# Loading batch 3's x earlier, and a new order around batch 2's scores and normalisation

## The chip, the core and the metric

The kernel runs on one core of a Trainium2 chip. The core has four engines that compute: TensorE (PE in the profile; PEld is its weight load), VectorE (DVE), ScalarE (ACT) and GpSimd (POOL). SyncE (SP) computes nothing here; it issues DMAs, as GpSimd and ScalarE also do. Each engine takes its own instructions strictly in order, and waits for the others by semaphores. TensorE writes its results to PSUM, of which the kernel uses two pools of four banks; VectorE and ScalarE carry them on to SBUF.

The metric is the device time of one execution in microseconds. The kernel before takes 205.47 us, the median of six runs (205.08 to 206.97).

## What is computed

Two blocks follow each other: a cross attention between a sequence and a small state, and a feed-forward layer with the exact GELU. Cut to what matters:

```python
B, H, S, Ns, D = 8, 8, 512, 32, 64
# x [B,H,S,D], state [B,H,Ns,D], w_in [512,2048], w_out [2048,512], all float32
a     = softmax(x @ state.T / sqrt(D))       # over the 32 states
xread = a @ state
a2    = softmax(state @ x.T / sqrt(D))       # over the 512 positions
sread = a2 @ x
X     = concat([xread, sread], axis=2)       # [B, H, S+Ns, D] -> [B*(S+Ns), H*D]
out   = gelu(X @ w_in) @ w_out               # [4352, 512]
```

## The kernel before

**What is tiled how.** Everything stays in bfloat16 between the steps. The work goes by batch, 0 to 7, 512 positions each. For a batch the kernel forms the transposed x (`xT`), multiplies it with the states (`scores`: 16 small matmuls in two halves, each followed by one exp on ScalarE), normalises on VectorE (`norm`: a sum, a reciprocal and a product for each half) and transposes the result (`AT`). It never forms xread: `p_mm` multiplies the states with w_in into `P` (by `f`, blocks of 512 columns), and the first layer is AT times P. `M(k)` (`mm1`) is one of its 128-column chunks of a batch: two matmuls into a PSUM tile `hp`, then one GELU on ScalarE into `g`. There are 16 chunks for a batch, so M(16) to M(31) belong to batch 1 and M(32) begins batch 2.

The second layer is `U` (`mm2`) for batch 0: output rows j, evacuated by VectorE into `osb` and written by SyncE. From batch 1 on it is `X`, a scheme with seven products over halves (named "1" to "7"), whose operands are sums of g (`g_sum`) or of w_out (`w_sums`), formed on VectorE.

**What sets the order.** The program is written out by hand. Each engine executes its instructions in the order in which they stand in the program, and waits are derived from the tiles. So a line's place decides what it stands behind on its engine, and the pools decide what it can wait for:

- `xin` has two buffers of `xb`, the loaded x: batch 3's x uses the buffer of batch 1, whose last readers are `xtr(1)` on TensorE and `rearr_ones(1)` on VectorE.
- `ps_f` is a ring of four PSUM banks (`ftile`): hp, the scores' `pt`, most P tiles and the transposed states pass through it in turn.
- `ps_o` has four banks named o0 to o3 (`otile`): the output rows of U and the products of X. X "3" and "5" share bank 0, "4" and "2" bank 1, "1" and "7" bank 2, and "6" has bank 3.

**The stage around the change** lies between the end of batch 0's second layer and the regular loop over batches 2 to 7 (L1112). There GpSimd's queue is: `load_rest` (the rest of the weights, the states of batch 2, the x of batch 2, and as the last piece w_out's chunks 12 to 15), then `rearr(2)` (two copies that arrange x into `x4`, the form that can be transposed by DMA), a small copy `hold_for(0, 15)` that makes the queue wait for a GELU of batch 0, `load_x(3)`, `load_st(3, B)` (the states of batches 3 to 7), `rearr(3, (0,))`, a copy that waits for batch 2's normalised scores, `rearr(3, (1,))`, another hold and `rearr_ones(2)`.

SyncE's queue is: `xtr_dma(2)` (the DMA that transposes x4 into xT), the writes of U(12) to U(15), `atr_dma(2)` (the transpose of batch 2's normalised scores `a` into AT), `xtr_dma(3)`.

TensorE's order is: M(18, 19), U(12), P for batch 1, U(13), states of batch 2, M(20, 21), U(14), M(22, 23), U(15), scores of batch 2, X(1, "3"), M(24) to M(27), X(1, "6"), P for batch 2 (`p0`, `p1`), M(28) to M(31), the transposed states of batches 3 to 7 (`state_prep(3, B)`, which needs `load_st(3, B)`), and then M(32).

On ScalarE two table loads stand around the exps of each batch: one from GELU to exp, one back.

Of the kernel before, what the change touches and what calls it, by code (L numbers as in the profile page):

```python
# [9 lines left out]
FP32 = mybir.dt.float32  # L10
BF16 = mybir.dt.bfloat16
AF = mybir.ActivationFunctionType
# [5 lines left out]
def kernel(  # L18
# [8 lines left out]
    nc = tc.nc  # L27
# [11 lines left out]
    persist = ctx.enter_context(tc.tile_pool(name="persist", bufs=1))  # L39
# [36 lines left out]
    xT0 = persist.tile([128, 4, SJ, 128], BF16, name="xT0", tag="mix2")  # L76
    sb0 = persist.tile([128, 2, 2, 2, NS], BF16, name="sb0")
    hold = persist.tile([128, 1], BF16, name="hold")
    warm = persist.tile([128, 512], BF16, name="warm")
    xos = [persist.tile([128, SJ, HC, 132], BF16, name=f"xo_{i}") for i in range(2)]  # L80
    x4s = [persist.tile([128, SJ, HC, 128], BF16, name=f"x4_{i}") for i in range(2)]
# [15 lines left out]
    for i in range(2):  # L97
        nc.vector.memset(xos[i][:, :, :, 1:2], 1.0)
        nc.vector.memset(xos[i][:, :, :, 130:131], 1.0)

    def load_w_in(f0, f1):
        for t in range(2):
            nc.gpsimd.dma_start(
                out=w_in_bf[64 * t:64 * t + 64, :, f0:f1],
                in_=moe_w_in[256 * t:256 * t + 256, f0:f1].rearrange("(c d) f -> d c f", c=HC),
            )
# [3 lines left out]
    def load_w_out(m0, m1):  # L110
        nc.gpsimd.dma_start(out=w_out_bf[:, m0:m1, :], in_=w_out_r[:, m0:m1, :])

    def load_x(b):
        xb = xin.tile([128, H, SJ * D], BF16, name="xb", tag="xb")
        nc.gpsimd.dma_start(out=xb, in_=xr[b])
        xbs[b] = xb

    def load_st(b0, b1):
        nc.gpsimd.dma_start(
            out=st_bf[:, b0:b1, :, :].rearrange("q b t d -> q (b t) d"),  # L120
            in_=st_rows[:, b0:b1, :, :].rearrange("q b t d -> q (b t) d"),
        )
# [9 lines left out]
    def load_rest():  # L132
        load_w_out(4, 6)
        load_w_out(6, 8)
        load_w_in(1024, 1536)
        load_w_out(8, 12)
        load_w_in(1536, 2048)
        load_st(2, 3)
        load_x(2)
        load_w_out(12, 16)  # L140


    def keep_warm(n):
# [57 lines left out]
    atts = {}  # L201

    def begin(b):
        A = Att()
        atts[b] = A
        A.x4 = x4s[b % 2]
        A.xo = xos[b % 2]
        if b > 0:
            A.xT = att.tile([128, SJ, HC, 128], BF16, name="xT", tag="xT")
# [8 lines left out]
    def rearr(b, ts=(0, 1)):  # L218
        A = atts[b]
        src = xbs[b].rearrange("p (t c) (j d) -> p t c j d", t=2, d=D)  # L220
        for t in ts:
            nc.gpsimd.tensor_copy(  # L222
                out=A.x4[:, :, :, 64 * t:64 * t + 64].rearrange("p j c d -> p c j d"),
                in_=src[:, t],
            )
# [47 lines left out]
    def xtr_dma(b):  # L273
        A = atts[b]
        nc.sync.dma_start_transpose(
            out=A.xT.rearrange("p j c n -> p (j c) n"),
            in_=A.x4.rearrange("p j c n -> p (j c n)"),
        )
# [29 lines left out]
    def norm0(t):  # L308
        A = atts[0]
        ics = att.tile([128, SJ, HC], FP32, name="ics", tag="ics")  # L310
        nc.vector.reciprocal(out=ics, in_=A.sums)
        nc.vector.tensor_tensor(
            out=A.a.rearrange("p (j t) (c n) -> p j t c n", t=2, n=NS)[:, :, t, :, :],
            in0=A.e.rearrange("p (j t) (c n) -> p j t c n", t=2, n=NS)[:, :, t, :, :],
            in1=ics[:, :, :].to_broadcast((128, SJ, HC, NS)),
            op=ALU.mult,
        )

    def scores(b, half):
        A = atts[b]  # L320
        if half == 0:
            begin_e(b)
        pt = ps_f.tile([128, SJ, 2, 2, NS], FP32, name="pt", tag="f")
        for ci in range(2):
            c = 2 * half + ci
            for j in range(SJ):
                nc.tensor.matmul(  # L327
                    pt[:, j, :, ci, :],
                    lhsT=A.xT[:, j, c, :],
                    rhs=sbd[:, b, c, :],  # L330
                    start=True,
                    stop=True,
                )
        nc.scalar.activation(  # L334
            out=A.e[:, :, 64 * half:64 * half + 64],
            in_=pt.rearrange("p j t c n -> p (j t) (c n)"),
            func=AF.Exp,
            scale=scale,
        )
# [75 lines left out]
    Ps = {}  # L415
# [128 lines left out]
    def w_add(name, x, y, op):  # L544
        if name == "3":
            pair = persist.tile([128, 2, MH, NH], BF16, name="ws_34", tag="mix0")
            w_sum["3"], w_sum["4"] = pair[:, 0], pair[:, 1]
        elif name != "4":
            tag = {"6": "mix1", "1": "mix2", "7": "mix3"}[name]
            w_sum[name] = persist.tile([128, MH, NH], BF16, name=f"ws_{name}", tag=tag)  # L550
        nc.vector.tensor_tensor(out=w_sum[name], in0=x, in1=y, op=op)

    def w_sums(i):
        (b11, b12), (b21, b22) = w_q
        w_add(*(
            ("3", b12, b22, ALU.subtract),
            ("4", b21, b11, ALU.subtract),
            ("6", b11, b12, ALU.add),
            ("1", b11, b22, ALU.add),
            ("7", b21, b22, ALU.add),  # L560
        )[i])
# [14 lines left out]
    def g_sum(b, name):  # L576
        (h0, k0), (h1, k1), op = G_SUMS[name]
        t = apool.tile([128, MH, 256], BF16, name="gsum", tag="gsum")
        nc.vector.tensor_tensor(out=t, in0=g_q(b, h0, k0), in1=g_q(b, h1, k1), op=op)  # L579
        xs[b, "g" + name] = t  # L580
# [34 lines left out]
    def X(b, name):  # L615
        bank = {"3": 0, "4": 1, "5": 0, "2": 1, "1": 2, "6": 3, "7": 2}[name]
        first = name in "3416"
        if first:
            xs[b, bank] = otile([128, 2, NH], "xp", bank)
        ps = xs[b, bank]  # L620
        lhs = {"3": (0, 0), "4": (1, 1)}.get(name)
        lhs = xs[b, "g" + name] if lhs is None else g_q(b, *lhs)
        rhs = {"5": w_q[1][1], "2": w_q[0][0]}.get(name)
        rhs = w_sum[name] if rhs is None else rhs
        x_mm(ps, lhs, rhs, first)
        if name == "3":
            xs[b, "s3"] = c_tile("s3")
            if b > 1:
                nc.scalar.copy(out=xs[b, "s3"], in_=ps)
            for h in range(2):  # L630
                xs[b, "o", h] = hpool.tile([128, 2, d_model], FP32, name="oh", tag=f"oh{h}")
        elif name == "4":
            xs[b, "s34"] = c_tile("s34")
            nc.vector.tensor_tensor(out=xs[b, "s34"], in0=ps, in1=xs[b, "s3"], op=ALU.add)
        elif name == "5":
            o = xs[b, "o", 0][:, :, NH:]
            nc.scalar.copy(out=o, in_=ps)  # L637
            xs[b, "u"] = c_tile("u")
            x_out(b, 0, right)
            nc.gpsimd.tensor_tensor(out=xs[b, "u"], in0=xs[b, "s34"], in1=o, op=ALU.subtract)  # L640
        elif name == "2":
            nc.scalar.copy(out=xs[b, "o", 1][:, :, :NH], in_=ps)  # L642
            c22(b)
        elif name == "1":
            xs[b, "q"] = c_tile("q")
            nc.vector.tensor_tensor(out=xs[b, "q"], in0=ps, in1=xs[b, "s34"], op=ALU.add)
        elif name == "7":
            nc.vector.tensor_tensor(
                out=xs[b, "o", 0][:, :, :NH], in0=ps, in1=xs[b, "u"], op=ALU.add
            )  # L650
            x_out(b, 0, left)
# [253 lines left out]
    def hold_for(b, m):  # L905
        nc.gpsimd.tensor_copy(out=hold, in_=gs[b][:, m, 0:1])


    def M(*ms):
        for m in ms:  # L910
            mm1(m // MC, m % MC)

    def U(*us):
        for u in us:
            mm2(u // 16, u % 16 // 4, u % 4)
# [146 lines left out]
    begin(2)  # L1062
    rearr(2)
    xtr_dma(2)
    hold_for(0, 15)
    load_x(3)
    load_st(3, B)
    M(18, 19)
    U(12)
# [1 line left out]
    U(13)  # L1071
    state_prep(2, 3, ps_o, "o3")
    w_sums(1)
    begin(3)
    rearr(3, (0,))
    M(20, 21)
    U(14)
    M(22, 23)
    g_sum(1, "6")
    U(15)  # L1080
    scores(2, 0)
    scores(2, 1)
# [1 line left out]
    norm(2, 0)  # L1084
    norm(2, 1)
    atr_dma(2)
    nc.gpsimd.tensor_copy(out=hold, in_=atts[2].a[:, 0, 64:65])
    rearr(3, (1,))
    xtr_dma(3)
    M(24, 25)  # L1090
    M(26, 27)
    X(1, "6")
    homes = iter((1, 2, None, None))

    def home(shape, name):
        at = next(homes)
# [1 line left out]

    p0 = p_mm(2, 0, home)
    p1 = p_mm(2, 1, home)  # L1100
    for f, t, ps in ((1, 0, p1), (1, 1, p1), (0, 1, p0)):
        nc.vector.tensor_copy(out=Ps[2][:, t, f * 512:(f + 1) * 512], in_=ps[t])
    M(28, 29)
    nc.scalar.copy(out=Ps[2][:, 0, 0:512], in_=p0[0])
    hold_for(1, 12)
    rearr_ones(2)
    M(30, 31)
    state_prep(3, B)
    nc.scalar.copy(out=xs[1, "s3"], in_=xs[1, 0])
    w_sums(3)  # L1110

    for b in range(2, B):  # L1112
# [122 lines left out]
```

The softmax here doesn't subtract the row's maximum and nothing guards it: scores larger than these inputs give would overflow.

## Time and profile before

| | |
|---|---|
| median of six runs | 205.47 us |
| the profiled execution | 205.34 us |
| its span in the profile | 203.6 us |
| granted TensorE clock | 1.00 throughout |
| DMA queue of GpSimd's loads (casting float32 to bfloat16) | 13984 packets, 8.10 MB |
| DMA queue of SyncE's writes and transposes | 25872 packets, 14.36 MB |
| HBM read, written | 17.30 MB, 8.91 MB |
| GELU on ScalarE, 128x512 | 124 of them, 602 ns each |
| table load on ScalarE | 1283 ns each |
| sum of two g blocks on VectorE, 128x2048 | 35 of them, 1326 ns each |
| rearranging copy on GpSimd, 128x1024 | 12 of them, 1081 ns each |
| x of one batch, from issue to landing | median 6.0 us |
| DMA transpose of x, of a, to landing | median 4.4 us, 3.7 us |

In the profile a line of a timeline gives the start, the length, the engine with the source line, the operation with its tiles (output <- input), and in brackets the idle time before it with what ended it. Starts are more exact than ends on TensorE, since matmuls are pipelined and their ends are modelled. A chain of waits is followed back from the last instruction to what released each step; its lines give start, length and what it was. The span is the time in which the engines run; the rest of the 205.34 us lies around it.

### The profile page before, as it was taken

The page shows a single profiled execution, that of the slowest core. Times are in us where ns is not written, and L with a number is a line of the kernel's source. Part 1 is how long each engine was busy: PE and PEld are TensorE (multiplying, and loading weights), DVE is VectorE, ACT ScalarE, POOL GpSimd, SP SyncE. Part 2 cuts the span into 40 slices and gives each one's busy share as a digit, 9 for nine tenths or more (in the row PEclk, how much of TensorE's full clock was granted, in tenths as well). Part 3 has the DMA queues.
Part 4 walks back from the last instruction along what each step waited for, and adds up shares of the span by engine and source line. Part 5 has one row for each costly group of instructions (what it writes and reads, how often), then busy time and mean ns, then how long its engine had stood idle before and what let it go on. Part 6 is the DMA issues. An engine that isn't in the chain of part 4 may idle for free.

```text
span 203.6 us, 4900 instructions
## 1 busy us (share of the span) xinstructions
PE 196.6 (97%) x2035; PEld 132.6 (65%) x2035; DVE 157.2 (77%) x254; ACT 135.4 (67%) x239; POOL 68.0 (33%) x76
## 2 busy tenths in 40 slices
PE   7699999999899999999999999999999999999994
PEld 2333544465577567766776677667776787878893
DVE  2773777688998988977897787768778988895882
ACT  3685677678986679565967697587847576864120
POOL 8972303323529546370626602330220002200000
PEclk9999999999999999999999999999999999999999
DMA  6999996994785798745583405750107001040135
GB/s 195 189 191 191 197 199 108 148 223 125 120 143 106 190 122 104 158 156 53 70 170 127 104 0 117 105 148 0 52 3 206 3 0 55 0 155 3 52 101 162
DMA packets 40566, 23.16 MB, mean 114 GB/s; under 512 B 21856, under 2 KB 39136, under 8 KB 40544
## 3 DMA queue, kind: packets, MB, share of 16 engines
q0 software_dynamic: 13984, 8.10, 29.7%
q1 hardware_dynamic: 25872, 14.36, 28.5%
q10 hardware_dynamic: 688, 0.39, 0.6%
q8 instruction: 16, 0.26, 0.5%
q14 instruction: 6, 0.05, 0.1%
HBM read 17.30 MB, written 8.91 MB: 129 GB/s over the span
## 4 chain that ended last, share of the span: by engine, by line
PE 89%; DMA 5%; ACT 3%; DVE 1%; issue 1%; SPq 0%
PE xp L585 39%; PE hp L488 25%; PE op L530 5%; PE p_ps L423 4%; PE sp L792 3%; PE rp L858 3%; DMA x0f<-in_x_dram 3%; PE xp L697 2%; PE op L514 2%; DMA AT<-a 2%; PE pt L327 1%; PE sr L386 1%; ACT g L495 1%; PE hp L1003 1%; ACT L495 1%; ACT L334 1%
## 5 line engine op out<-in xcount | busy, mean ns | idle before, releaser
L495 ACT ACTIVATE g<-hp 128x512 bf16<-128x512 f32 x124 | 67.3, 602 | 27.4 <-PE hp L488 20.8
L488 PE MATMUL hp<-AT,P 128*128 128x512 bf16 x248 | 63.0, 379 | 0.7 <-DMA AT<-a 0.7
L585 PEld LDWEIGHTS <-gsum 128*128 128x128 bf16 x528 | 51.0, 98 | 12.4 <-issue 1.9
L579 DVE TENSOR_TENSOR gsum<-g 128x2048 bf16<-128x2048 bf16 x35 | 45.9, 1326 | 0.1
L488 PEld LDWEIGHTS <-P 128*128 128x128 bf16 x248 | 22.8, 98 | 21.4 <-issue 3.2
L585 PE MATMUL xp<-ws,gsum 128*128 128x256 bf16 x304 | 36.3, 273 | 0.0
L585 PE MATMUL xp<-ws,g 128*128 128x256 bf16 x224 | 26.8, 273 | 0.0
L585 PE MATMUL xp<-w_out_bf,gsum 128*128 128x256 bf16 x224 | 26.6, 273 | 0.0
L585 PEld LDWEIGHTS <-g 128*128 128x128 bf16 x224 | 21.7, 98 | 4.6 <-issue 0.2
L640 POOL TENSOR_TENSOR u<-s,oh 128x512 f32<-128x512 f32 x6 | 8.9, 1490 | 40.7 <-ACT oh L637 40.7
L435 DVE CAST P<-p_ps 128x512 bf16<-128x512 f32 x29 | 18.8, 684 | 3.0 <-PE p_ps L423 2.9
L222 POOL COPY x<-xb 128x1024 bf16<-128x1024 bf16 x12 | 12.7, 1081 | 20.7 <-DMA xb<-in_x_dram 20.7
L434 ACT CAST P<-p_ps 128x512 bf16<-128x512 f32 x29 | 15.8, 598 | 5.4 <-PE p_ps L423 5.1
L232 POOL COPY xo<-xb 128x1024 bf16<-128x1024 bf16 x12 | 14.6, 1246 | 4.5 <-PE sr L386 4.5
L604 POOL TENSOR_TENSOR v<-q,oh 128x512 f32<-128x512 f32 x6 | 8.7, 1456 | 20.5 <-ACT oh L642 20.3
L530 PE MATMUL op<-w_out_bf,g 128*128 128x512 bf16 x48 | 11.8, 380 | 0.0
L350 DVE TENSOR_TENSOR a<-e,ics 128x512 bf16<-128x512 bf16 x14 | 10.4, 739 | 0.5
L347 DVE TENSOR_REDUCE cs<-e 128x16 f32<-128x512 bf16 x14 | 9.5, 677 | 1.1 <-ACT e L334 1.1
L423 PE MATMUL p_ps<-w_in_bf,sbd 64*32 64x512 bf16 x248 | 10.3, 382 | 0.0
L413 DVE COPY XSR<-srT 128x128 bf16<-128x128 bf16 x8 | 5.7, 757 | 5.3 <-PE srT L410 5.3
L334 ACT ACT_TABLE_LOAD x7 | 9.0, 1283 | 0.6 <-issue 0.5
L495 ACT ACT_TABLE_LOAD x7 | 9.0, 1283 | 0.1
(129 smaller groups left out, 225.0 us busy)
## 6 DMA issues: line engine op xcount, KB each, us to landing
out_dram<-oh SPq DMA_DIRECT2D x15, 256.0 KB, 2.8
xb<-in_x_dram POOLq DMA_DIRECT2D x7, 512.0 KB, 6.0
out_dram<-oh SPq DMA_DIRECT2D x6, 512.0 KB, 3.1
w_in_bf<-in_moe_w_in_dram POOLq DMA_DIRECT2D x6, 256.0 KB, 11.6
out_dram<-osb SPq DMA_DIRECT2D x5, 256.0 KB, 4.5
w_out_bf<-in_moe_w_out_dram POOLq DMA_DIRECT2D x4, 256.0 KB, 8.3
w_out_bf<-in_moe_w_out_dram POOLq DMA_DIRECT2D x2, 512.0 KB, 13.2
x0f<-in_x_dram SPq DMA_DIRECT2D x3, 256.0 KB, 3.9
```

What stands on the lines that cost most here:

```text
L222: nc.gpsimd.tensor_copy(out=A.x4[:, :, :, 64 * t:64 * t + 64].rearrange("p j c d -> p c j d"), in_=src[:, t],)
L232: eng.tensor_copy(out=A.xo[:, :, :, 2 + 64 * t:66 + 64 * t].rearrange("p j c d -> p c j d"), in_=src[:, t],)
L334: nc.scalar.activation(out=A.e[:, :, 64 * half:64 * half + 64], in_=pt.rearrange("p j t c n -> p (j t) (c n)"), func=AF.Exp, scale=scale,)
L350: nc.vector.tensor_tensor(out=A.a[:, :, hs].rearrange("p g (c n) -> p g c n", n=NS), in0=e4, in1=ics[:, :, :].to_broadcast((128, G, 2, NS) ...
L423: nc.tensor.matmul(ps[t][32 * c:32 * c + 32, :], lhsT=sbd[64 * t:64 * t + 64, b, c, 32 * t:32 * t + 32], rhs=w_in_bf[64 * t:64 * t + 64, c ...
L434: nc.scalar.copy(out=dst[:, 0, :], in_=ps[0])
L435: nc.vector.tensor_copy(out=dst[:, 1, :], in_=ps[1])
L488: nc.tensor.matmul(hp, lhsT=Ps[b][:, t, m * 128:(m + 1) * 128], rhs=atts[b].AT[:, :, t, :], start=(t == 0), stop=(t == 1),)
L495: nc.scalar.activation(out=gs[b][:, m, :], in_=hp, func=AF.Gelu)
L530: nc.tensor.matmul(ops[b, j], lhsT=gs[b][:, m, j * 128:(j + 1) * 128], rhs=w_out_bf[:, m, :], start=(m == 0), stop=(m == MC - 1),)
L579: nc.vector.tensor_tensor(out=t, in0=g_q(b, h0, k0), in1=g_q(b, h1, k1), op=op)
L585: nc.tensor.matmul(ps[:, j - js[0], :], lhsT=lhs[:, m, 128 * j:128 * j + 128], rhs=rhs[:, m, :], start=(first and j == js[0] and m == 0), ...
```

## The change

There are five parts. The load of batch 3's x moves from behind the hold to the end of `load_rest`, so that it is the next thing in GpSimd's queue after the last w_out piece; all of `rearr(3)` follows `rearr(2)` at once, and the states of batches 3 to 7 now stand behind a one-element copy that reads batch 2's xT. The transpose of batch 3's x is issued by SyncE between the writes of U(14) and U(15), no longer behind `atr_dma(2)`. M(22, 23) come ahead of U(14), and behind their GELUs stands a new exp of one element per partition (`exp_table` on `spare`). `g_sum(1, "6")` moves behind batch 2's normalisation on VectorE, and `X(1, "6")` behind the transposed states on TensorE. The four P tiles of batch 2 get other banks (three of ps_o and one of the ring), and ScalarE casts the last of them and VectorE the other three.

```diff
+    spare = persist.tile([128, 1], FP32, name="spare")
...
+    nc.vector.memset(spare, 0.0)
...
         load_st(2, 3)
         load_x(2)
         load_w_out(12, 16)
+        load_x(3)
...
+    def exp_table():
+        nc.scalar.activation(out=spare, in_=spare, func=AF.Exp)
...
     begin(2)
     rearr(2)
     xtr_dma(2)
-    hold_for(0, 15)
-    load_x(3)
+    begin(3)
+    rearr(3)
+    nc.gpsimd.tensor_copy(out=hold, in_=atts[2].xT[:, 0, 0, 0:1])
     load_st(3, B)
     M(18, 19)
     U(12)
...
     U(13)
     state_prep(2, 3, ps_o, "o3")
     w_sums(1)
-    begin(3)
-    rearr(3, (0,))
     M(20, 21)
+    M(22, 23)
+    exp_table()
     U(14)
-    M(22, 23)
-    g_sum(1, "6")
+    xtr_dma(3)
     U(15)
     scores(2, 0)
     scores(2, 1)
...
     norm(2, 0)
     norm(2, 1)
     atr_dma(2)
-    nc.gpsimd.tensor_copy(out=hold, in_=atts[2].a[:, 0, 64:65])
-    rearr(3, (1,))
-    xtr_dma(3)
+    g_sum(1, "6")
     M(24, 25)
     M(26, 27)
-    X(1, "6")
-    homes = iter((1, 2, None, None))
+    homes = iter((1, 3, 2, None))
...
     p0 = p_mm(2, 0, home)
     p1 = p_mm(2, 1, home)
-    for f, t, ps in ((1, 0, p1), (1, 1, p1), (0, 1, p0)):
+    nc.scalar.copy(out=Ps[2][:, 1, 512:1024], in_=p1[1])
+    for f, t, ps in ((0, 1, p0), (0, 0, p0), (1, 0, p1)):
         nc.vector.tensor_copy(out=Ps[2][:, t, f * 512:(f + 1) * 512], in_=ps[t])
     M(28, 29)
-    nc.scalar.copy(out=Ps[2][:, 0, 0:512], in_=p0[0])
     hold_for(1, 12)
     rearr_ones(2)
     M(30, 31)
     state_prep(3, B)
     nc.scalar.copy(out=xs[1, "s3"], in_=xs[1, 0])
+    X(1, "6")
     w_sums(3)
```

## The prediction

> **What bounds the kernel now.** I read the page's busy shares first, then who waited for whom on the PE, then the chain of work in order of time around the changed stage. From the page:
>
> ```profile
> PE 196.6 (97%) x2035; PEld 132.6 (65%) x2035; DVE 157.2 (77%) x254; ACT 135.4 (67%) x239; POOL 68.0 (33%) x76
> ```
>
> The PE (TensorE) is the bound, nearly without a gap. The list of PE waits has four lines; all but one lie in the first 15 us. The one in the steady part:
>
> ```profile
> PE hp L488 <- DMA AT<-a: 0.7, 1, 0.7
> ```
>
> The chain from 38 to 58 us shows where it sits (start, length, what):
>
> ```profile
> 42.60 0.47 issue
> 43.07 1.28 ACT L334
> 44.35 0.01 issue
> 44.37 1.08 ACT e L334 x2
> 45.45 0.02 issue
> 45.47 1.28 ACT L495
> 46.75 0.01 issue
> 46.76 1.70 ACT g L495 x4
> 48.47 3.35 DMA AT<-a
> 51.82 0.04 issue
> 51.86 1.02 PE hp L488 x4
> ```
>
> For 9 us the chain leaves the PE: batch 2's scores end, ACT waits, loads the exp table (1.28), runs two exps, AT is transposed by DMA, and only then can M(32) start. From 45.47 to 48.47 it names ACT's GELUs, which run beside it; the transpose really waits for VectorE's normalisation, by its timeline:
>
> ```profile
> 45.00 0.69 DVE L347 TENSOR_REDUCE cs<-e 128x16 f32<-128x512 bf16 x1 [0.54 <-ACT e L334]
> ...
> 47.61 0.69 DVE L350 TENSOR_TENSOR a<-e,ics 128x512 bf16<-128x512 bf16 x1
> ```
>
> Meanwhile the PE's own work is, by the starts in its timeline:
>
> ```profile
> 42.60 0.63 PE L327 MATMUL pt<-sbd,xT 128*128 128x64 bf16 x16
> 43.07 1.91 PE L585 MATMUL xp<-ws,g 128*128 128x256 bf16 x16
> 44.82 1.89 PE L488 MATMUL hp<-AT,P 128*128 128x512 bf16 x8
> 46.55 1.91 PE L585 MATMUL xp<-ws,gsum 128*128 128x256 bf16 x16
> 48.38 0.63 PE L423 MATMUL p_ps<-w_in_bf,sbd 64*32 64x512 bf16 x16
> 48.94 1.90 PE L488 MATMUL hp<-AT,P 128*128 128x512 bf16 x8
> 50.68 0.44 PE L157 MATMUL st_ps<-ident,st_bf 128*128 128x128 bf16 x5
> 51.86 1.02 PE L488 MATMUL hp<-AT,P 128*128 128x512 bf16 x4 [0.74 <-DMA AT<-a]
> ```
>
> Read the starts, since the ends overlap. Five transposes issue 0.06 apart, so M(32) could start at 50.68 + 0.30 = 50.98 and starts at 51.86: **0.88 us** lost (0.74 counted from the modelled end). No matmul is removed or added by the change. After 51.86 the chain stays on the PE, back to back, to about 200 us. So 0.74 to 0.88 us is the most this stage can give.
>
> **The change, part by part.**
>
> *Exp table earlier.* M(22,23) move ahead of U(14), so their hp starts at 40.02, not 40.88. ACT ran GELU 20 at 39.78 and 21 at 0.49 later (four take 2.06, so 0.49 apart and 0.60 long): GELU 22 at 40.76, 23 at 41.25, done 41.84. exp_table's load takes 1.28 (to 43.14). Its 128x1 exp is not in the trace; the rows 128x256 (375 ns) and 128x512 (587) give 0.84 ns an element and leave about 0.16 fixed: 43.30. Before, the load itself stood behind an ACT queue wait for the scores (41.9 for 1.094 us, to 43.0); now only the exp waits for them, and 43.0 is past. So exp 0 starts at 43.32 instead of 44.37: **1.05 earlier**. "ScalarE: Activation LUTs", section What ACT_TABLE_LOAD costs, puts a drain of about 1.38 us on top of the 1283 ns load; here exp starts 0.02 after the load (44.35 to 44.37), so I take the row. By the rule 2.4 us would leave the chain; the PE could use no more than 0.88 either way.
>
> *g_sum(1,"6") behind the normalisation.* VectorE's osb copy of U(15) (0.69) then starts when the PE is done, about 42.8, and ends by 43.5, before exp 0 ends (43.91). Normalisation took 45.00 to 48.30, 3.30; now 43.95 to 47.25. SyncE issued AT 0.17 later, so 47.42, and with the same 3.35 it lands at **50.77**; with the 3.7 median of six such transposes at 51.1. Against 50.98 that is a stall of 0 to 0.14.
>
> *X(1,"6") behind state_prep(3).* Same matmuls, but p_mm and M(28..31) come 1.83 us earlier on the PE, where ACT must keep up. With exps at 43.32 and 43.81, the GELU table is loaded by 45.70; GELU 24 to 27 end 46.31, 46.80, 47.29, 47.77, the ACT cast of p1 48.25. In the ring of four PSUM tiles p1's one ring tile needs GELU 24 (PE there at 46.83), M(28) to M(31) need GELU 25, 26, 27 and the cast, with the PE there at 47.11, 47.54, 47.98, 48.41: slack 0.52, 0.31, 0.25, 0.21, 0.16. Cost nothing; if ACT is 0.4 later, about 0.25. X(1,"6") is reached at 49.15 and needs gsum (DVE 47.2 to 48.4) and bank 3, freed by the first P cast (48.4 to 49.1). Without cover: a gsum beside a GpSimd copy takes 1.98 (3.97 for two at 77.52) instead of 1.22, which would stall X by about 0.7. GpSimd's next copies wait for GELU 28 (about 48.8), so I take none. All four P casts remain, three on DVE, one on ACT; the first two are done by 49.7, before M(32).
>
> *x of batch 3 early.* The load's buffer is batch 1's, free after rearr_ones(1) on DVE (24.03); GpSimd is idle there until rearr(2) at 32.37, so issue (0.9) and wait hold up nobody. It queues behind w_out's last piece. The rate in the window 30 to 36 us (40 slices of 0.15):
>
> ```profile
> GB/s 212 201 208 205 208 191 201 208 212 198 208 208 208 218 198 164 137 109 123 123 116 102 68 82 82 68 27 27 27 14 0 0 0 0 0 0 55 2 138 213
> ```
>
> From 32.4 the tail moves 0.17 MB: 0.8 us at 200 GB/s, so x (0.52 MB, 2.6 us) is through at about 36 to 37.5. Before it landed at 44.09. The DMA engines sat idle from 34.5 to 35.4, which it fills. w_out comes first in the queue and keeps its time.
>
> *Beside x^T of batch 2.* Issued 34.42, landing 4.4 later (38.8), wanted by the PE's weight load at 42.39: 3.6 us of slack. "DMA: Bandwidth & Descriptors", section Queues, rings and completion order, speaks against the overlap: each DMA engine takes turns between queues packet by packet. By it x^T waits for at most all of x, 38.8 + 2.6 = 41.4; by the row 38.8. Both under 42.39: no cost. The trace has no x^T beside a load; the nearest mixed case, the osb writes beside batch 3's x, took 6.6 us instead of about 3.
>
> *rearr(3), hold, states, x^T of batch 3.* rearr(3) (two copies, 2.0) ends about 39.5, the hold (0.19) waits for x^T of batch 2, at worst 41.4; load_st issues by then (0.95). It took 9.1 to land behind x; by itself it is between 2.4 us (0.16 MB at 200 GB/s, 0.8, and a load's start, 1.6: batch 4's x is issued at 53.79 and moves from 55.4) and the 6.0 of an x three times its size: 42 to 47.6, wanted at 48.85. On SyncE, x^T of batch 3 stands behind U(14)'s write (42.62 + 0.35), takes 1.7 to 2.7, then U(15)'s two writes (0.36 each) follow and are issued by 46.4, 1.0 before AT. It lands near 48. That also matters: before, issued at 49.80, it landed at about 54.1, with batch 3's scores at 54.91; behind an earlier M(32) this would have been next to wait. The memset of spare (72 ns class) lies under the first loads.
>
> **Sum.** Profiled run 205.34 (span 203.57). Removed 0.88 at most; left over 0 to 0.14 for AT, 0 to 0.25 for ACT's pace: net -0.5 to -0.9, I take **-0.8**. Against the median of 205.47: **204.65 us**, range of this case 204.4 to 205.0. That is 0.4%; 0.5% (1.03 us) is about what a measurement of this kernel tells from no change.
>
> **Rivals.**
> 1. *The new order paces the PE by ACT or DVE.* For: the slacks above are 0.1 to 0.3 us and each rests on modelled ends. Against: ACT idled 0.76 before GELU 28 and moves 1.05 forward. Then 0.4 to 0.9 of the gain goes: 205.1 to 205.5. Chance 0.20.
> 2. *Slower: x^T of batch 2 stretched by x.* For: the doubling of the osb writes. Doubled, 34.42 + 8.8 = 43.2 stalls the scores by 0.8 and eats the gain (205.5). It decides from a landing at 44.3 on, 10 us after issue: 1.9 us of stall less 0.85 is +1.05, so 206.5 and more. Against: x should be through soon after x^T's first packets at 35.4. Chance of over +0.5%: 0.12. States landing past 48.85, or x so late that its transpose blocks AT on SyncE (rearr(3) after 43.8), would look the same: 0.04 more.
> 3. *The load does not come forward* (buffer or queue order holds it): with the rest of the change it lands near 44 at the earliest only if issued near 36; then rearr(3), transpose and AT collide on SyncE, about +1 to +2, 206.5 to 207.5. Against: the buffer's last reader ends at 24.03. Chance 0.02.
> 4. *More than the counted stall* (under -0.5%): 0.22, out of noise around -0.44% and small gaps hidden in modelled ends.
>
> Main case within 0.5%: 0.40. So faster 0.22, same 0.40 + 0.20 = 0.60, slower 0.18. The range takes the main case, rival 4 and rival 1, and a little of 2: 204.2 to 205.9.
>
> **What would show it.** Right: the PE waits list without AT; exp table load at about 41.9 and exp 0 near 43.3; AT issued about 47.4; x of batch 3 landed before 39; M(32) at 51.0 to 51.1, and every later start on the PE earlier by the same amount. Wrong: PE idle at the scores (xT), at st_ps (states), at M(28..31) (ACT) or at X(1,"6") (DVE), or M(32) still waiting for AT because SyncE was still issuing batch 3's x^T.

## The result and the profile after

The changed kernel takes 204.39 us in the median of 36 runs (203.53 to 205.56), the kernel before 205.22 in 73 runs taken beside it and earlier (204.32 to 208.03). The ratio is 0.9958, 95% interval 0.9944 to 0.9971: 0.4% faster. A second measurement with its own runs of before gave 0.9962 (0.9941 to 0.9982).

The profiled execution took 204.68 us, span 202.9. PE's busy row and its waits in the steady part of the changed kernel:

```profile
PE 196.4 (97%) x2035; PEld 132.4 (65%) x2035; DVE 156.7 (77%) x255; ACT 135.4 (67%) x240; POOL 67.5 (33%) x75
```

```profile
PE hp L494 <- DMA AT<-a: 0.7, 1, 0.7
```

The wait that the change was to remove is still there, and as long as before. The chain of waits over the same stage (start, length, what):

```profile
42.08 0.47 PE pt L333 x16
42.55 1.75 PE xp L591 x16
44.29 1.73 PE hp L494 x8
46.02 0.63 PE p_ps L429 x16
46.65 0.03 ACTq L1104
46.68 0.35 ACT g L501
47.02 0.03 ACT P L1104
47.06 3.97 DMA AT<-a
51.02 0.14 issue
51.16 1.02 PE hp L494 x4
```

Compare it with the chain of before. The table load is gone from it, and so are the exps. AT stands in it for 3.97 us instead of 3.35 and is issued at 47.06. On TensorE's own timeline the last work ahead of M(32) is X(1, "6"):

```profile
41.92 0.63 PE L333 MATMUL pt<-sbd,xT 128*128 128x64 bf16 x16
...
48.52 1.91 PE L591 MATMUL xp<-ws,gsum 128*128 128x256 bf16 x16
51.16 1.02 PE L494 MATMUL hp<-AT,P 128*128 128x512 bf16 x4 [0.72 <-DMA AT<-a]
```

Sixteen matmuls 0.109 apart are through at 50.27, so M(32) loses 0.89 us, against 0.88 before. From the first score matmul to M(32), which I call **the stretch**, it is 51.16 - 41.92 = 9.24 us; before it was 9.26. The 0.7 us between the two profiled spans is there when the stretch begins: its start is 41.92 in one and 42.60 in the other.

So a median that fell by the forecast 0.8 us stands beside a profile in which the stage did not shrink. The experiments ask how the two go together.

### The profile page after: what moved, and what is told of

The parts are those of the page before. It is cut to its first block, busy times and chain, and to the rows that moved or that the text cites. A ratio compares the mean times of both kernels' runs of the same rounds, so it can differ in the third digit from the quotient of the medians.

```text
span 202.9 us, 4899 instructions
## 1 busy us (share of the span) xinstructions
PE 196.4 (97%) x2035; PEld 132.4 (65%) x2035; DVE 156.7 (77%) x255; ACT 135.4 (67%) x240; POOL 67.5 (33%) x75
## 4 chain that ended last, share of the span: by engine, by line
PE 83%; DMA 12%; POOL 3%; issue 0%; ACT 0%; DVE 0%; POOLq 0%; ACTq 0%
PE xp L591 40%; PE hp L494 24%; DMA w_out_bf<-in_moe_w_out_dram 10%; PE p_ps L429 4%; PE sp L798 3%; PE rp L864 3%; DMA AT<-a 2%; PE op L536 2%; PE op L520 2%; PE xp L703 2%; PE pt L333 1%; POOL w_in_bf L105 1%; PE sr L392 1%; POOL sbd L95 1%; POOL st_bf L121 0%; POOL w_out_bf L113 0%
## 5 line engine op out<-in xcount | busy, mean ns | idle before, releaser
L618 DVE TENSOR_TENSOR oh<-xp,v 128x512 f32<-128x512 f32 x6 | 4.1, 690 | 5.2 <-POOL v L610 5.2
```

## The experiments

An execution differs from the next by about 1 us before the stage: over 14 profiles of all versions the last piece of batch 0's x lands between 6.1 and 7.8 us, the first matmul of the first layer starts between 10.31 and 11.71, and batch 2's scores between 41.41 and 42.60. From M(32) on, the way to the batch that reads the states out takes 109.1 us in twelve of them and 109.3 in two. So single executions are compared from the first score matmul on: by the stretch, and by **the whole way** to the start of VectorE's last operation. Kernels are compared by the ratio of their times.

| kernel | ratio to before, 95% | stretch | whole way | normalisation ends | AT issued |
|---|---|---|---|---|---|
| before (three profiles) | 1 | 9.26, 9.54, 9.26 | 157.96, 158.23, 157.95 | +5.70 (first) | +5.87 (first) |
| changed (three profiles) | 0.9958, 0.9962 | 9.24, 9.26, 9.58 | 157.94, 157.97, 158.28 | +4.58 | +5.14, +5.24, +5.29 |
| order_only | 0.9960 (0.9939 to 0.9980) | 8.98 | 157.89 | +5.45 | +5.61 |
| load_only | 0.9995 (0.9980 to 1.0010) | 9.02 | 157.93 | +5.70 | +5.86 |
| load_late_xT3 | 0.9984 (0.9968 to 1.0001) | 9.26 | 157.95 | +5.70 | +5.86 |
| xT3_behind_AT | 0.9928 (0.9904 to 0.9952) | 8.35 | 157.07 | +4.58 | +4.74 |
| late_again (the same kernel) | 0.9948 (0.9930 to 0.9966) | 8.35 | 157.06 | +4.58 | +4.74 |
| late_no_exp | 0.9991 (0.9966 to 1.0016) | 9.31 | 158.00 | +5.70 | +5.86 |
| xT3_before_U14 | 0.9952 (0.9937 to 0.9968) | 8.51 | 157.25 | +4.59 | +4.75 |
| U15w_behind_AT | 0.9962 (0.9939 to 0.9984) | 9.57 | 158.27 | +4.58 | +4.74 |

All columns but the ratio count from the first score matmul, in us.

### The changed kernel and the kernel before, again

> The changed kernel once more, for a second profile. In the first pair of profiles the stretch from the first score matmul of batch 2 to M(32) is 9.26 us before and 9.24 after, although the median fell by 0.4%; the 0.68 us between the two spans is there before that stretch begins. Theory 1 (the wait for AT is what the change shortens): the first profile was an unlucky one, and this one shows the stretch at 8.4 to 9.0 us. Theory 2 (the stretch is unchanged, the gain lies earlier): 9.2 us again. Ratio to before 0.994 to 0.998 by both.

> The kernel before, for a second profile. Its first profile has one x load at the very start landing after 6.1 us where four later profiles of other versions have 4.5 to 4.7, so its scores of batch 2 start at 42.60 and theirs at 41.65 to 42.34. If the stretch from the scores to M(32) explains the medians, it is 9.2 us or more here and the whole difference to the changed kernel must lie in it or behind it; if it is 9.26 again with scores at 41.7, the run should take about 204.5 us.

> The same, a third profile: how far start, stretch and rest of the kernel before vary between executions.

> The changed kernel, a third profile. Stretch 9.24 and 9.26 us so far. Theory (the wait for AT is behind the transpose of batch 3's x on SyncE and varies with when that transpose gets its descriptors through): between 8.4 and 9.3 us. Rival (constant): 9.25.

The second profile of the changed kernel has the stretch at 9.26 and the same wait, so theory 1 in its plain form (the change shortens the wait) missed. The third has 9.58, longer than either theory had it: AT was issued at +5.29 and took 4.15 us to land, at 51.49, and M(32) started at 51.63. Its TensorE waits:

```profile
PE st_ps L160 <- DMA st_bf<-in_state_dram: 0.5, 1, 0.5
PE hp L494 <- DMA AT<-a: 0.4, 1, 0.4
```

The states, loaded behind batch 2's x^T, were late too, but that cost M(32) nothing: what TensorE waited for them it waited the less for AT. M(32) starts at 51.16, 51.60 and 51.63 in the changed kernel and at 51.86, 51.78 and 51.80 before; the profiled times (204.68, 205.10, 205.03 against 205.34, 205.28, 205.30) follow that. Before, the scores start at 42.60, 42.24 and 42.54; with the change at 41.92, 42.34 and 42.05. The whole way is the same in both kernels, so all that their profiled times differ by lies ahead of the scores.

### The order alone, the load alone

order_only takes the changed kernel and puts the loads and the transpose back:

```diff
         load_w_out(12, 16)
-        load_x(3)
...
-    begin(3)
-    rearr(3)
-    nc.gpsimd.tensor_copy(out=hold, in_=atts[2].xT[:, 0, 0, 0:1])
+    hold_for(0, 15)
+    load_x(3)
     load_st(3, B)
...
+    begin(3)
+    rearr(3, (0,))
     M(20, 21)
...
-    xtr_dma(3)
     U(15)
...
     atr_dma(2)
+    nc.gpsimd.tensor_copy(out=hold, in_=atts[2].a[:, 0, 64:65])
+    rearr(3, (1,))
+    xtr_dma(3)
```

> The new order on TensorE, ScalarE and VectorE, with the loads, rearr(3) and batch 3's transpose where they were before (behind AT). Theory 1: the normalisation ends 1.05 us earlier as in the changed kernel and no transpose of x stands in front of AT on SyncE, so AT lands in time: 204.4 to 204.7, ratio about 0.996, stretch 8.4 to 8.7 us. Rival (the early load and the place of the transpose bring the gain): ratio 0.999 to 1.001, stretch 9.2.

load_only takes the kernel before and moves the load, rearr(3), the states and batch 3's transpose to their new places.

> Batch 3's x, rearr(3), the states and batch 3's transpose at their new places, with the order on TensorE, ScalarE and VectorE of before. Theory 1: the normalisation ends where it did, so M(32) waits as before or longer, since U(15)'s writes are held behind the transpose on SyncE: ratio 0.999 to 1.003, stretch 9.2 to 9.8 us. Rival: ratio about 0.996.

By the ratios the order alone gives the whole 0.4%, the load with its transpose nothing that can be measured. load_only's stretch, 9.02, is shorter than was expected: there the normalisation ends 1.1 us later, when SyncE is free again, and AT landed after 3.12 us. Its whole way is that of before all the same; 0.2 us are lost again behind M(32).

order_only's own stretch is 8.98 and not 8.4 for a reason that is worth seeing. Here are VectorE's second product of the normalisation, the GpSimd copy of batch 3's x, which starts when that x lands, and X(1, "6") on TensorE with what it waits for:

```profile
45.62 1.56 DVE L355 TENSOR_TENSOR a<-e,ics 128x512 bf16<-128x512 bf16 x1
```

```profile
45.60 1.04 POOL L224 COPY x<-xb 128x1024 bf16<-128x1024 bf16 x1 [7.74 <-DMA xb<-in_x_dram]
```

```profile
48.97 1.91 PE L590 MATMUL xp<-ws,gsum 128*128 128x256 bf16 x16 [0.47 <-DVE P L1108]
```

The product starts 0.02 us behind the copy and takes 1.56 instead of 0.69; g_sum and P's first cast stand behind it on VectorE, and X(1, "6") waits for that cast, which frees its bank. In before's second profile the copy starts at 45.05, the first product 0.59 behind it takes 0.99, the normalisation ends at +6.00, and the stretch is 9.54. A second wait follows in order_only, behind M(32), for batch 3's x^T, which is issued at 49.36 and lands at 53.91, just ahead of its scores:

```profile
PEld L332 <- DMA xT<-x: 0.3, 1, 0.3
```

The prediction had named this one as next to wait. It takes back 0.2 us, so that order_only's whole way is that of before within 0.1. The late load therefore has a price of its own.

### The transpose behind AT

```diff
     U(14)
-    xtr_dma(3)
     U(15)
...
     atr_dma(2)
+    xtr_dma(3)
     g_sum(1, "6")
```

> The changed kernel with batch 3's transpose issued behind AT and not ahead of U(15)'s writes. In the changed kernel's profile the first of these writes took 2.33 us to issue, AT was issued 0.56 us behind the normalisation (0.17 before) and landed 3.97 us later (3.35 before). Theory 1 with this loss: AT is issued within 0.2 us and lands in 3.4, stretch 8.4 to 8.7 us, ratio to before 0.993 to 0.996, no slower than the changed kernel; batch 3's scores (12.3 us after those of batch 2) still find xT. Rival (AT's landing isn't set by what is in front of it): AT lands as late as in the changed kernel, and the time is the same or longer by a wait for xT.

> The version with batch 3's transpose behind AT once more, beside the others on one chip. If it beats both kernels: ratio to before 0.991 to 0.995, stretch 8.35 to 8.5 us, no wait for AT. If the first measurement was luck: 0.996 like the changed kernel.

This is the changed kernel with one line moved, and the fastest kernel of the study: 203.74 us in the median where the changed kernel beside it has 204.64 (14 executions from 203.35 to 204.33, 22 from 203.87 to 205.44), and 203.97 in the second measurement, where xT3_before_U14 below has 203.79: these two are not told apart. Both intervals to before lie below 1 by more than 0.3%; against the changed kernel itself there are these times alone, without an interval. TensorE waits for nothing in the stage, and the whole way is 0.9 us shorter than before in both profiles. The chain of waits of xT3_behind_AT:

```profile
45.86 0.56 PE p_ps L429 x16
46.41 1.83 PE hp L494 x8
48.25 0.28 PE st_ps L160 x5
48.53 1.75 PE xp L591 x16
50.27 0.86 PE hp L494 x4
```

Its stretch of 8.35 us is what the prediction worked out for TensorE without a wait (50.98 - 42.60 = 8.38). SyncE's queue shows what stood in the way. First the changed kernel, its issues in order, with the two writes of U(15) apart:

```profile
42.41 1.57 SPq L278 DMA_TRANSPOSE xT<-x  x1
44.08 2.33 SPq L509 DMA_DIRECT2D out_dram<-osb  x1
46.46 0.42 SPq L509 DMA_DIRECT2D out_dram<-osb  x1
47.06 1.34 SPq L381 DMA_TRANSPOSE AT<-a  x1
```

then the version with the transpose behind AT, the two writes of U(15) in one line:

```profile
42.68 0.83 SPq L509 DMA_DIRECT2D out_dram<-osb  x2
46.50 1.25 SPq L381 DMA_TRANSPOSE AT<-a  x1
47.84 1.96 SPq L278 DMA_TRANSPOSE xT<-x  x1
```

The other writes of U cost 0.3 to 0.6 us to issue; the one right behind batch 3's transpose took 2.33, 2.44 and 2.34 in the three profiles of the changed kernel. In the changed kernel the normalisation ended at 46.50, and SyncE could take AT only at 47.06. That is 0.40 of what AT lost against xT3_behind_AT (+5.14, not +4.74); the other 0.63 is its landing, 3.97 instead of 3.34.

### Without the early exp table

```diff
     M(22, 23)
-    exp_table()
     U(14)
```

taken from the version with the transpose behind AT.

> The version with batch 3's transpose behind AT, without the early exp table load. Theory 1: the exps start about 1.0 us later, the normalisation ends 1.0 later, AT lands that much later, M(32) waits 0.6 to 0.9 us and also M(28..31) run closer behind ScalarE: stretch 8.9 to 9.4 us, ratio to before 0.996 to 0.998 where the version with it has 0.9928. Rival (the table load is hidden anyway): 0.993.

The normalisation ends at +5.70 instead of +4.58, the stretch is 9.31 instead of 8.35, and the gain is gone (0.9991). But no wait for AT is listed. TensorE loses the time earlier, at P: its matmuls start at 45.45 and M(28) at 46.71, 1.26 us where the other version has 0.56, since P's ring tile waits for GELUs that ScalarE now runs later; M(28) to M(31) lose about 0.2 more. The size is that of theory 1, the place is not: it is the pacing by ScalarE that the prediction's rival 1 named.

### The early load by itself

load_only with its transpose moved behind AT:

```diff
-    xtr_dma(3)
     U(15)
...
     atr_dma(2)
+    xtr_dma(3)
```

> The early load alone: order on TensorE, ScalarE and VectorE as before, batch 3's transpose behind AT as before. Theory 3 (the late x collides: in the kernel before, GpSimd's copy of batch 3's x starts when x lands, at 44.1 to 45.6 us, and where a product of the normalisation starts beside it that product takes 0.99 or 1.56 us instead of 0.69, so that an execution with an early start loses it again): no such product is long, stretch 9.2 to 9.3 us whatever the start, ratio 0.996 to 0.999. Rival (the early load is worth nothing by itself): 0.999 to 1.001, as load_only, whose transpose stood in front of U(15)'s writes.

No product is long and the stretch is 9.26. The ratio, 0.9984 with an interval that ends at 1.0001, leans to theory 3 and does not decide it. Its profile has the whole way of before. With the new order the early load looks worth more, 0.9928 and 0.9948 with it, 0.9960 without it, but the intervals overlap.

### What delays AT: the write, or the transpose's traffic

xT3_before_U14 moves `xtr_dma(3)` one line up, ahead of `U(14)`. U15w_behind_AT leaves the transpose where the change has it and writes U(15)'s output by one DMA behind AT:

```diff
+    last = []
...
         if q == 3:
             rows = out_rows(b, j)
+            if j == SJ - 1:
+                osb = opool.tile([128, d_model], FP32, name="osb", tag="osb")
+                nc.vector.tensor_copy(out=osb, in_=ps)
+                last.append((rows, osb))
+                return
...
     atr_dma(2)
+    nc.sync.dma_start(out=last[0][0], in_=last[0][1])
```

> The changed kernel with batch 3's transpose one step earlier on SyncE, ahead of U(14)'s write. Theory (what delays AT is the write of U(15) that stands right behind a transpose in SyncE's queue and takes 2.3 us to issue): now U(14)'s write is the long one, 3 us earlier, AT is issued within 0.2 us of the normalisation and lands in 3.4 to 3.7; stretch 8.4 to 8.7, ratio 0.992 to 0.995. Rival (the transpose's traffic delays AT, wherever it stands): stretch 9.0 to 9.3, ratio 0.996.

> The changed kernel with U(15)'s output written by one DMA of 256 KB that is issued behind AT; batch 3's transpose stays where the change has it. Theory (the writes behind the transpose): AT is issued within 0.2 us of the normalisation and lands in 3.4 to 3.7, stretch 8.4 to 8.7, ratio 0.992 to 0.995. Rival (the transpose's own traffic): AT is issued in time but lands in 4 us or more, stretch 8.9 to 9.2.

With the transpose earlier, the write behind it (U(14)'s) takes 1.31 us, AT goes out in time and lands after 3.1, and TensorE does not wait for it: 8.51 us, 0.9952. So the long write is what held SyncE. But U15w_behind_AT shows that it is not all. AT is issued in time at +4.74, lands after 3.75 us (between what the theory and the rival had) and TensorE does not wait for it, and yet the stretch is 9.57. Its chain of waits runs through DMAs only:

```profile
34.16 6.87 DMA xT<-x
41.03 0.05 issue
41.08 0.19 POOL hold L1079
41.27 0.05 issue
41.32 7.85 DMA st_bf<-in_state_dram
49.17 0.05 issue
49.22 0.45 PE st_ps L160 x5
```

Batch 2's x^T, beside the load, lands after 6.87 us; the hold lets the states go only then; and they take 7.85 us to land beside batch 3's transpose. TensorE waits 1.0 us for them. In xT3_before_U14 the states, issued at 40.99, took 7.2 us and held TensorE by 0.16 us, which is its whole difference to 8.35.

AT's landing goes with batch 3's transpose: where that one was in flight for 2 us or more behind AT's issue (the changed kernel and U15w_behind_AT), AT took 3.75 to 4.15 us, in the ten other profiles 3.09 to 3.36. No run parts this from the other transfers of the time.

## Why the prediction was right, and where its steps failed

**The size was right, but the profiles do not confirm how it came about.** Forecast 204.65, measured 204.39 in the first and 204.64 in the second measurement. The forecast rested on M(32) no longer waiting for AT, and in all three profiles of the changed kernel the stretch is as long as before; as far as these show, the agreement is luck. The limit of 0.88 us from TensorE's work, and that the rest of the kernel is unmoved, hold once AT has SyncE's queue to itself: 8.38 worked out, 8.35 measured, and 109.1 us from M(32) to the reading out, before and after.

**Exp table: right.** The spare exp took 0.20 us (0.16 estimated), exp 0 starts 0.66 us behind the first score matmul (0.72 forecast, 1.77 before). No drain is seen behind the table load here either: 41.18 + 1.28 = 42.46, and the spare exp begins at 42.47. late_no_exp prices it: 0.96 us of stretch.

**Normalisation: right.** It ends at +4.58 (forecast 47.25 - 42.60 = 4.65; before 5.70).

**AT: wrong, and this is the step that failed.** The prediction had U(15)'s two writes at 0.36 each behind the transpose of batch 3's x, issued by 46.4, AT 0.17 behind the normalisation and 3.35 to 3.7 to land: +8.17 to +8.5. The first write took 2.33; AT went out at +5.14 and landed after 3.97, at +9.10, and "left over 0 to 0.14 for AT" was 0.89. Two terms were mis-sized. The long write used up the 1.0 us of slack on SyncE and held AT 0.32 longer than forecast; the landing was 0.62 longer than the 3.35 taken, 0.27 longer than the 3.7. The prediction named "SyncE still issuing batch 3's x^T" as a way to fail; it was the write behind it, and AT's own landing.

**X(1, "6") behind the states: right.** No matmul of p_mm, M(28) to M(31) or X(1, "6") waits in the first two profiles of the changed kernel.

**x beside batch 2's x^T: the rule was nearer than the row.** I took 38.8 from the row, a landing after 4.4 us, and 41.4, after 7.0, as my estimate from the Trainium skill's rule that a DMA engine takes turns between queues packet by packet ("DMA: Bandwidth & Descriptors", Queues, rings and completion order). Measured, by the DMA issues of the window in which it goes out, the kernel before and then the changed one (median us to landing at the end):

```profile
xT<-x SPq DMA_TRANSPOSE x1, 4.4
```

```profile
xT<-x SPq DMA_TRANSPOSE x1, 6.6
```

It landed at 41.4, for a weight load at 41.7. Batch 2's x^T is stretched as rival 2 had it; that came 0.3 us short of costing anything.

**States: too optimistic at its end.** Forecast 42 to 47.6 and slack of over 1 us; they landed after 6.3 us at 48.05 in the first profile, 0.2 ahead of their use, and 0.5 too late in the third, where AT was later still.

**x itself: nearly right.** It landed at 37.92; 36 to 37.5 was the forecast, and a landing before 39 the sign of being right.

**What stays open.** Where the 0.4% is saved. By the ratios the order is its source. But all three profiles of the changed kernel have the stretch and the whole way of before, and what they save lies ahead of the scores, where the two kernels do the same work on TensorE and where the kernels of every other run also vary. order_only and U15w_behind_AT are the same case: 0.4% by the ratio, and no gain in the whole way. The three versions without the early exp table gain little or nothing by either measure, and the two with it that free AT gain by both. It would fit that unprofiled executions with the early exp table wait less than the profiled ones (in the changed kernel two profiled executions took 0.3 and 0.5 us more than the medians of their runs), or that the kernel before loses an early start to the copy that collides with its normalisation, which was seen in one of three profiles. Neither is shown to account for the 0.8 us.

## What to carry to other kernels

When a transfer is moved earlier on a queue, price not only its own issue but the next one behind it, and look for the transfer that ends the critical wait in the same queue: here one line moved behind it was worth another 0.1 to 0.3% by the ratios. A number that comes out right does not confirm the steps; the wait list of the new profile showed at once that this one had not gone. And compare executions stage by stage, since a start that varies by 1 us hides a gain of 0.8.

## What the runs showed of the hardware that was not expected

- A plain write that SyncE issues right behind batch 3's transpose (128x2048 bfloat16) took 1.31 to 2.44 us to issue in five profiles, the other writes of U 0.33 to 0.57. Not every write behind a transpose is held: U(12)'s stands right behind batch 2's, whose own issue took 3.17 us in the changed kernel, and took 0.57.
- A VectorE product of two SBUF operands that starts beside a GpSimd copy of 1.04 us is held up by it: started 0.02 us behind the copy it took 1.56 us instead of 0.69, started 0.59 behind it 0.99. In both cases it ended 0.54 us after the copy.
- The states of five batches, 160 KB in pieces of 64 elements, take 4.7 to 6.0 us to land with neither batch 3's x nor its transpose beside them (four profiles), and 6.2 to 7.9 with the transpose (six).
